# All matmuls of the main part of a fused attention and MLP layer as concurrent pairs of 64-row tiles

## The chip, the cores and the metric

The kernel runs on one core of one Trainium2 chip. The metric is the device time of one execution in microseconds (us). Each figure below is the median of several executions. A core has a TensorE (PE), which does the matmuls and writes to eight PSUM banks, and three elementwise engines: VectorE (DVE), ScalarE (ACT) and GpSimd (POOL). SyncE (SP) issues most DMAs.

## The reference, cut to what matters

```python
# S=2048 tokens, D=448, H=16 heads of Dh=28, F=1792
def _A_ref(x, wqkv, w_phi, wo):                      # linear attention
    q, k, v = ...(x @ wqkv)...
    pq = einsum("bhsd,hdf->bhsf", q, w_phi)          # pk likewise from k
    phi_q = concatenate([softmax(pq), softmax(-pq)]) # phi_k likewise
    kv  = einsum("bhsf,bhsd->bhfd", phi_k, v)        # "K-V"
    z   = einsum("bhsf->bhf", phi_k)
    num = einsum("bhqf,bhfd->bhqd", phi_q, kv)       # "numerators"
    den = einsum("bhqf,bhf->bhq", phi_q, z)[..., None] + 1e-6
    return (num / den)... @ wo

def _B_ref(x, w1, w2, w3, w4):                       # MLP with token shifts
    h  = gelu(layernorm(x) @ w1)
    hs = concatenate([four column blocks of h, shifted by 1, -1, 2, -2 tokens]) @ w2
    x1 = x + hs
    return x1 + gelu(layernorm(x1) @ w3) @ w4

xn = layernorm(x)
return x + _A_ref(xn, ...) + _B_ref(xn, ...)
```

## The kernel before

The kernel is one long unrolled program. A recorder takes every operation with what it reads and writes, and sets the semaphore waits: counters that hold an instruction back until the work it needs is done. Tokens are in 16 tiles of 128. D=448 is 3.5 times 128, so a product over D takes three matmuls with 128 rows (the contraction dimension lies on the rows) and one with 64. The 64-row ones, the *tails*, are issued in pairs on the upper and the lower half of the PE array, where they run at the same time (in the trace a pair's starts lie 3 ns apart).

The program has four stages:

1. The first 33.5 us or so: layer norm, transposes, V and W1 products. The change leaves them alone.
2. The K/Q loop, eight passes, from about 34 to 79 us. A pass makes K and Q products for two tiles and their exps on ACT. Then it makes W2 products, which DVE adds into `xn`, and K-V products of K tiles that DVE and POOL have normalised.
3. From the first W3 product on: the output stage. W3 products, Gelu on ACT, numerators, the division on DVE and POOL, a DMA transpose of the result `o`, and the W4 and `wo` products. DVE adds the residual ("fin_out").
4. The last two output tiles, in 128-row form before and after.

```python
def fulls(p, first, fills=()):            # 128-row matmuls
    for k in range(4):
        for kc in (0, 3, 2 - k % 2):
            R.mm(outs(k), lhs(k, kc, 0, 128), rhs(k, kc, 0, 128), ...)
        ...
def tails(p, first):                      # 64-row matmuls, even k rows 0-63, odd k rows 64-127
    for k in range(4):
        kc, lo = 1 + k % 2, 64 * (k % 2)
        R.mm(outs(k), lhs(k, kc, lo, lo + 64), rhs(k, kc, lo, lo + 64), first, not first)
def quad(p, fills=(), more=()):           # four banks: K/Q products, or W3 products
    fulls(p, True, fills)
    tails(p, False)
    for f in more: f()
def kv_tile(i):                           # 128 tokens on the rows
    for c in range(NC):
        R.mm(banks[6 + c // 2][...], vaug[:, i, 128*c:128*c+128], phik[:, i, :, CR*c:CR*c+CR], ...)
def num_tile(i):                          # 4 heads x 28 = 112 rows, 4 x 32 = 128 columns out
    for s in range(2):
        for c in range(NC):
            R.mm(bs[s][:, 128*c:128*c+128], eqT(g, c, s, ...), kvq[0:CR, 2*c+s, :], True, True)
    ...                                   # reciprocals, multiplies: DVE, then POOL
def fin_full(i):                          # 14 W4 and 3 wo matmuls with 128 rows; fin_tail(i): the 64-row one
    ...
plan = [ ...,
    [(N, 1), (O, 1), (Ff, 0), (G, 8), (G, 9), (N, 2), (O, 2)],   # what runs behind W3 quad 4
    ... ]
```

The softmax here doesn't subtract the row's maximum and nothing guards it: scores larger than these inputs give would overflow.

Of the kernel before, what the change touches and what calls it, by code (L numbers as in the profile page):

```python
# [17 lines left out]
class Recorder:  # L18
# [47 lines left out]
    def op(self, eng, fn, outs, ins, dma=False):  # L66
        w = set()
        r = set()
        for a in outs:
            w.update(self._keys(a))  # L70
        for a in ins:
            r.update(self._keys(a))
        self.ops.append((eng, fn, w, r, dma))

    def solve(self):
# [8 lines left out]
        for eng, fn, w, r, dma in self.ops:  # L84
# [21 lines left out]
            for k in w:  # L106
                if k in writers:
                    want(writers[k], False)
                if k in readers:
                    want(readers[k], False)  # L110
            kn = known[eng]
# [74 lines left out]

    def mm(self, out, lhsT, rhs, start, stop):
        self.op("PE", lambda e: e.matmul(out, lhsT, rhs, start=start, stop=stop, skip_group_check=True),  # L188
                [out], [lhsT, rhs])

    def tr(self, out, in_, ident):
        self.op("PE", lambda e: e.transpose(out, in_, ident), [out], [in_, ident])  # L192
# [16 lines left out]
def bass_parallel_sum__linear_kernel_hedgehog__mixer_s_mlp__prompt_kernel(  # L209
# [13 lines left out]
    with es:  # L223
# [42 lines left out]
        wpq = new("wpq", KC * D).rearrange("p (c d) -> p c d", c=KC)  # L266
# [8 lines left out]
        kvq = new("kvq", 8 * 128).rearrange("p (b e) -> p b e", b=8)  # L275
        kvT = view(w1_r, NC * 224).rearrange("p (c f) -> p c f", c=NC)
# [32 lines left out]
        def eqT(g, c, sgn, lo, hi):  # L309
            e = eq_lo if g < 2 else eq_hi  # L310
            return e[0:CR, c, sgn, 512 * (g % 2) + lo:512 * (g % 2) + hi]
# [49 lines left out]
        kq = kvq[0:CR, :, :].rearrange("p b (h e) -> p b h e", e=HP)  # L361
# [24 lines left out]
        def late_3():  # L386
            R.ew(pool, "memset", kvq[0:CR, :, :], 0.0)
            for b in range(8):
                R.ew(pool, "tensor_copy", kq[:, b, :, DH + 1:DH + 2], mb[:, :, 0:1])
# [47 lines left out]
        def fold(t, m, b):  # L437
            b = banks[b]
            for c in range(NC):
                R.mm(b[:, CR * c:CR * c + CR], wT[0:CR, t, c, START[m]:START[m] + 128], bd[0:CR, CR * c:CR * c + CR], True, True)  # L440
            dst = wpq if t == 0 else wpk
            R.ew(dve, "tensor_copy", dst[:, m, :], b[:, 0:D])
# [68 lines left out]
        def kq_quad(i, bs):  # L511
            g, c = divmod(i, 4)

            def outs(k):
                return banks[bs[k]][:, 0:D] if k < 2 else banks[bs[k]][0:CR, :]

            def lhs(k, kc, lo, hi):
                if k < 2:
                    return xnT[lo:hi, kc, 128 * (i + k):128 * (i + k) + 128]
                return wpq[lo:hi, kc, CR * (c + k - 2):CR * (c + k - 1)]  # L520

            def rhs(k, kc, lo, hi):
                return wpk[lo:hi, kc, :] if k < 2 else xnT[lo:hi, kc, 512 * g:512 * g + 512]

            quad((outs, lhs, rhs))
            for s in range(2):
                R.act(phik[:, i:i + 2, s, :], two(bs[0])[:, :, 0:D], ACT.Exp, scale=1.0 - 2.0 * s)
            e = (eq_lo if g < 2 else eq_hi)[0:CR, c:c + 2, :, 512 * (g % 2):512 * (g % 2) + 512]
            for s in range(2):
                R.act(e[:, :, s, :], two(bs[2])[0:CR, :, :], ACT.Exp, scale=1.0 - 2.0 * s)  # L530
# [10 lines left out]
        def kv_tile(i):  # L541
            for c in range(NC):
                R.mm(banks[6 + c // 2][:, 224 * (c % 2):224 * (c % 2) + 224].rearrange("p (s f) -> p s f", s=2),
                     vaug[:, i, 128 * c:128 * c + 128], phik[:, i, :, CR * c:CR * c + CR],
                     i == 0 and c % 2 == 0, i == NT - 1)

        def kv_copy():
            for h in range(2):
                R.ew(dve, "tensor_copy", kvT[:, 2 * h:2 * h + 2, :],
                     banks[6 + h][:, 0:448].rearrange("p (c f) -> p c f", c=2))  # L550

        def kv_blocks():
            b = banks[6]
            tv = tview(b, 1024).rearrange("p (b e) -> p b e", b=8)
            for c in range(NC):
                for s in range(2):
                    R.tr(tv[0:CR, 2 * c + s, :], kvT[:, c, CR * s:CR * s + CR], ident[:, :])
            R.ew(dve, "tensor_tensor", kq[:, :, :, 0:DH + 1],
                 tv[0:CR, :, :].rearrange("p b (h e) -> p b h e", e=HP)[:, :, :, 0:DH + 1],
                 mb[:, :, 0:1].unsqueeze(1).to_broadcast([CR, 8, 4, DH + 1]), op=ALU.mult)  # L560

        def w2_tile(i, b=None, stats=True):
            b = bank(4, 5) if b is None else banks[b]
            for m in range(NM):
                c0 = 2 + 128 * i - SHIFTS[m]
                R.mm(b[:, 0:D], hT[0:CR, m, c0:c0 + 128], w2[0:CR, m, :], m == 0, m == NM - 1)
            R.ew(dve, "tensor_tensor", xn[:, i, 0:256], b[:, 0:256], xn[:, i, 0:256], op=ALU.add)
            R.ew(dve, "tensor_tensor", xn[:, i, 256:D], b[:, 256:D], xn[:, i, 320:512], op=ALU.add)
            if stats:
                ln_stats(st2, mv2, xn, i)  # L570
# [8 lines left out]
        def num_tile(i):  # L579
# [3 lines left out]
            for s in range(2):  # L583
                for c in range(NC):
                    R.mm(bs[s][:, 128 * c:128 * c + 128], eqT(g, c, s, 128 * j, 128 * j + 128),
                         kvq[0:CR, 2 * c + s, :], True, True)
# [24 lines left out]
        def w3_quad(q, more=()):  # L611
            gf = [divmod(4 * q + k, FC) for k in range(4)]
            quad((lambda k: banks[k][:, :],
                  lambda k, kc, lo, hi: w3[lo:hi, kc, 128 * gf[k][1]:128 * gf[k][1] + 128],
                  lambda k, kc, lo, hi: gT[lo:hi, gf[k][0] % 2, kc, :]), (), more)
            for k in (0, 2):
                g, fc = gf[k]
                R.act(h3T[:, g % 2, fc:fc + 2, :], two(k), ACT.Gelu_apprx_tanh)
# [4 lines left out]
        def fin_bank(i):  # L623
            return (0 if i > 13 else 6 if i > 11 else 4) + i % 2

        def fin_full(i):
# [5 lines left out]
            for kc in (0, 3, 2 - i % 2, 1 + i % 2) if i >= NT - 2 else (0, 3, 2 - i % 2):  # L632
                R.mm(b[:, 0:D], oT[:, g % 2, kc, 128 * j:128 * j + 128], wo[:, kc, :], False, kc == 1 + i % 2)

        def fin_tail(i):
            g, j = divmod(i, 4)
            kc, lo = 1 + i % 2, 64 * (i % 2)
            R.mm(banks[fin_bank(i)][:, 0:D], oT[lo:lo + 64, g % 2, kc, 128 * j:128 * j + 128], wo[lo:lo + 64, kc, :],
                 False, True)
# [36 lines left out]
        order = list("102" * 3 + "1021" + "021" * 3 + "012")  # L676

        def take(n):
            r = [int(order.pop(0)) for _ in range(n // 2)]
            return [2 * b + j for b in r for j in (0, 1)]  # L680

        w2s = {0: (0, 1, 2, 3), 1: (4, 5), 2: (6, 7), 4: (8, 9), 5: (10, 11), 6: (12,), 7: (13,)}
        kvs = {1: (0,), 2: (1,), 3: (2, 3), 4: (4, 5), 5: (6, 7), 6: (8, 9), 7: (10, 11, 12)}
        for ps in range(8):
            kq_quad(2 * ps, take(4))
            todo = [(kv_tile, i) for i in kvs.get(ps, ())]
            if ps > 1:
                todo[0][0](*todo.pop(0)[1:])
            if ps == 3:
                alone(v_parts(12, take(4)), (todo,))  # L690
            else:
                b = take(2)
                for i in w2s[ps]:
                    w2_tile(i, b[i % 2], False)
                    for f in todo[0:1]:
                        f[0](*f[1:])
                    todo = todo[1:]
                for f in todo:
                    f[0](*f[1:])
            k_norm(2 * ps)  # L700
            for i in w2s.get(ps, ()):
                ln_stats(st2, mv2, xn, i)
                if i % 4 == 3:
                    ln_scale(mv2, rs2, i - 3, 4, 4)
# [5 lines left out]
        N, W, O, G, St, Ff, Fo = num_tile, w2_tile, o_T, g_T, store, fin_full, fin_out  # L710

        def ga(g):
            for j in range(4):
                g_apply(4 * g + j)

        def sc(g):
            ln_scale(mv2, rs2, 4 * g, 4, 4)

        plan = [
            [(kv_tile, 13), (W, 14), (kv_tile, 14), (g_apply, 7)],  # L720
            [(kv_tile, 15), (kv_copy,), (W, 15), (sc, 3), (G, 4), (G, 5)],
            [(kv_blocks,), (G, 6), (G, 7), (ga, 2)],
            [(N, 0), (O, 0)],
            [(N, 1), (O, 1), (Ff, 0), (G, 8), (G, 9), (N, 2), (O, 2)],
            [(N, 3), (O, 3), (Ff, 1), (G, 10), (G, 11)],
            [(N, 4), (O, 4), (Ff, 2), (St, 0), (N, 5), (O, 5), (Ff, 3), (St, 1)],
            [(ga, 3), (N, 6), (O, 6), (Ff, 4), (St, 2), (St, 3)],
            [(N, 7), (O, 7), (Ff, 5), (G, 12), (G, 13), (G, 14), (G, 15)],
# [57 lines left out]
```

## Time and profile before

| | before |
|---|---|
| median of 4 runs | 194.83 us (194.8 to 195.46) |
| span on the core | 193.6 us |
| first K product to first W3 product | 44.87 us |
| first K product to last matmul | 156.36 us |
| time in it beyond steady streaming | 10.04 us |
| of this, 48 changes of tiling mode | 4.53 us |

The last two rows come from start-to-start distances. In steady streaming a matmul starts a fixed time after the one before it: 216 ns for 512 columns, 189 ns for 448, 96 ns for 224, 56 ns for 128. What a distance has beyond that is called a *gap* here. I use gaps because matmuls overlap in the pipeline, so "busy" doesn't mean "at its peak".

From the page of the kernel before, its size, the busy time of each engine, and the chain of work that ended last, by engine:

```profile
span 193.6 us, 2935 instructions
PE 186.2 (96%) x1137; PEld 94.2 (49%) x1137; DVE 114.1 (59%) x271; ACT 78.1 (40%) x88; POOL 96.4 (50%) x149
PE 78%; DVE 7%; POOL 7%; ACT 3%; DMA 3%; issue 1%; ACTq 0%; DVEq 0%
```

PE is the bound: it is busy 96% of the span and holds 78% of the chain. The timeline of PE in the kernel before shows where it streams below its peak. A line has the start in us, the time from the first start to the last end, the engine, the output and inputs, rows\*columns of the weights, rows x moving columns, and how many matmuls were merged.

```profile
41.47 1.46 PE L188 MATMUL bank<-xnT,wpq 128*112 128x512 bf16 x6
42.86 0.36 PE L188 MATMUL bank<-wpk,xnT 64*128 64x448 bf16 x2
43.06 0.38 PE L188 MATMUL bank<-xnT,wpq 64*112 64x512 bf16 x2
43.38 0.93 PE L188 MATMUL bank<-w,hT 112*128 112x448 bf16 x4
```

These are two changes of tiling mode. The last of the six Q matmuls started at 41.47 + 1.46 - 0.38 = 42.55. The first 64-row matmul starts at 42.86, so 0.31 us later instead of 0.216. The pair of Q tails starts at 43.06, the next 128-row matmul 0.32 us later. Each change costs about 95 ns (92 to 96 in 46 of the 48; the other two 90 and 104). The second excerpt is from the output stage:

```profile
114.14 0.62 PE L188 MATMUL bank<-kvq,eq_lo 112*128 112x128 bf16 x8
114.24 1.16 DVE L200 TENSOR_TENSOR vaug<-bank,vaug 128x448 bf16<-128x448 f32 x2 [4.21 <-PE bank L188]
114.92 0.55 PE L188 MATMUL bank<-w,phik 128*128 128x448 bf16 x2 [0.17 <-DVE vaug L200]
```

Eight numerator matmuls take (0.62 - 0.22) / 7 = 57 ns each (0.22 is the length of one). After them the W4 products wait for the DVE adds that empty their bank. This happened five times, and cost 0.33 us each in start-to-start distance. The waits view of PE counts only the idle part that the modelled ends leave:

```profile
PE bank L188 <- DVE vaug L200: 0.8, 5, 0.2
PE bank L188 <- ACT phik L196: 0.7, 2, 0.4
PE bank L188 <- ACT eq_lo L196: 0.3, 1, 0.3
PE bank L188 <- POOL phik L200: 0.3, 1, 0.3
```

(Columns: us in total, times, longest.) Together 2.1 us idle, beside 4.5 us of mode changes, which no view lists as a wait.

### The profile page before, as it was taken

To read this page: it belongs to the slowest core of one execution; us is meant where nothing else is said; L and a number is where in the kernel's file an instruction comes from. 1 tells how busy PE (TensorE), PEld (TensorE's weight loads), DVE (VectorE), ACT (ScalarE), POOL (GpSimd) and SP (SyncE) were. 2 spreads that over 40 slices of the span, in tenths; PEclk is the share of its full clock that TensorE was granted. 3 is DMA by queue.
4 is the path that set the end of the run, shared out by engine and by line. 5 is a ranking of instruction groups with operands and counts; after the bars stand their busy time and mean duration, and the time that the engine had idled before them with its cause. 6 is when DMAs were issued, how large, how long until landed. Compare 5 with 4: busy or idle time off the path is not lost.

```text
span 193.6 us, 2935 instructions
## 1 busy us (share of the span) xinstructions
PE 186.2 (96%) x1137; PEld 94.2 (49%) x1137; DVE 114.1 (59%) x271; ACT 78.1 (40%) x88; POOL 96.4 (50%) x149
## 2 busy tenths in 40 slices
PE   7899999999999999999899999999999999999994
PEld 5445555444445555454344545444454445464451
DVE  5699655399989999835356436154172626655031
ACT  2349836846774667844550440124210440404000
POOL 5567830017877979973524414940444124376140
PEclk9999999999999999999999999999999999999999
DMA  5994259920011110121011343302263021122211
GB/s 171 352 214 91 53 95 366 350 80 0 0 32 27 27 27 0 37 48 27 0 30 30 79 83 29 76 0 75 54 85 78 24 51 40 42 51 68 61 47 47
DMA packets 32971, 14.74 MB, mean 76 GB/s; under 512 B 24702, under 2 KB 32446, under 8 KB 32958
## 3 DMA queue, kind: packets, MB, share of 16 engines
q1 hardware_dynamic: 31710, 13.58, 29.5%
q10 hardware_dynamic: 1248, 0.98, 1.6%
q8 instruction: 9, 0.15, 0.3%
q14 instruction: 4, 0.03, 0.1%
HBM read 7.08 MB, written 1.84 MB: 46 GB/s over the span
## 4 chain that ended last, share of the span: by engine, by line
PE 78%; DVE 7%; POOL 7%; ACT 3%; DMA 3%; issue 1%; ACTq 0%; DVEq 0%
PE bank L188 77%; POOL phik L200 3%; DMA xtok<-in_A_x_dram 3%; ACT phik L196 2%; DVE vaug L200 2%; DVE st L200 2%; POOL rs L200 2%; DVE xn L200 1%; DVE ksum L200 1%; ACT eq_lo L196 1%; POOL mv L200 1%; DVE mv L200 1%; PE bank L192 1%; ACTq L206 0%; POOL xn L200 0%
## 5 line engine op out<-in xcount | busy, mean ns | idle before, releaser
L196 ACT ACTIVATE phik<-bank 128x1024 bf16<-128x1024 f32 (+1 forms) x44 | 41.0, 984 | 85.3 <-PE bank L188 85.3
L200 DVE TENSOR_TENSOR vaug<-bank,vaug 128x464 f32<-128x464 f32 (+3 forms) x65 | 32.7, 513 | 31.3 <-PE bank L188 29.7
L188 PE MATMUL bank<-gT,w 128*128 128x512 bf16 (+1 forms) x224 | 46.1, 380 | 0.7 <-ACT phik L196 0.7
L188 PE MATMUL bank<-w,phik 128*128 128x448 bf16 x224 | 45.1, 353 | 0.8 <-DVE vaug L200 0.8
L200 POOL TENSOR_TENSOR xnT<-vaug 128x196 bf16<-128x196 f32 (+1 forms) x32 | 18.1, 585 | 49.5 <-DVE vaug L200 49.5
L200 POOL TENSOR_TENSOR phik<-phik,rks 128x896 bf16<-128x896 bf16 x16 | 26.8, 1696 | 21.1 <-DVE rks L200 21.0
L188 PEld LDWEIGHTS bank<-w,phik 128*128 128x128 bf16 x224 | 21.0, 98 | 20.2 <-DVE vaug L200 1.7
L188 PEld LDWEIGHTS bank<-gT,w 128*128 128x128 bf16 (+1 forms) x224 | 17.7, 97 | 24.7 <-issue 5.9
L200 POOL TENSOR_TENSOR vaug<-xn,xtok 128x448 f32<-128x448 bf16 x16 | 16.4, 1031 | 5.1 <-DVE vaug L200 5.1
L200 DVE RECIPROCAL vaug<-bank 128x16 f32<-128x16 f32 x16 | 4.1, 254 | 22.7 <-PE bank L188 22.7
L200 DVE TENSOR_REDUCE ksum<-phik 128x32 f32<-128x896 bf16 x16 | 16.8, 1052 | 0.0
L188 PE MATMUL bank<-xnT,wpq 128*112 128x512 bf16 (+1 forms) x64 | 14.9, 381 | 0.3 <-ACT eq_lo L196 0.3
L188 PE MATMUL bank<-wo,xnT 128*128 128x448 bf16 (+1 forms) x64 | 14.5, 352 | 0.0
L188 PE MATMUL bank<-xnT,w 128*112 128x512 bf16 (+1 forms) x64 | 14.3, 383 | 0.0
L188 PE MATMUL bank<-w,hT 112*128 112x448 bf16 x64 | 14.3, 353 | 0.0
L200 DVE TENSOR_TENSOR xn<-bank,xn 128x256 bf16<-128x256 f32 (+1 forms) x32 | 10.6, 378 | 5.6 <-PE bank L188 5.4
L188 PE MATMUL bank<-wpk,xnT 128*128 128x448 bf16 (+1 forms) x64 | 13.3, 354 | 0.0
L188 PE MATMUL bank<-wv,xnT 128*128 128x448 bf16 (+1 forms) x64 | 12.7, 353 | 0.1
L200 POOL TENSOR_SCALAR g_tok<-xn,rs 128x512 bf16<-128x512 bf16 x16 | 12.1, 767 | 0.0
L200 POOL TENSOR_TENSOR rs<-mv,mhalf 128x1 f32<-128x1 f32 (+2 forms) x16 | 11.3, 705 | 1.3
L196 ACT ACTIVATE hT<-bank 112x1024 bf16<-112x1024 f32 x8 | 7.9, 1027 | 5.8 <-PE bank L188 5.7
L200 DVE BATCH_NORM_STATS2 st<-xtok 128x6 f32<-128x448 bf16 x16 | 9.8, 610 | 0.6 <-DMA xtok<-in_A_x_dram 0.6
(61 smaller groups left out, 178.4 us busy)
## 6 DMA issues: line engine op xcount, KB each, us to landing
w<-in_B_w_dram SPq DMA_DIRECT2D x2, 896.0 KB, 5.7
out_dram<-vaug SPq DMA_DIRECT2D x15, 112.0 KB, 1.9
w<-in_B_w_dram SPq DMA_DIRECT2D x1, 1568.0 KB, 12.1
xtok<-in_A_x_dram SPq DMA_DIRECT2D x2, 448.0 KB, 8.1
xtok<-in_A_x_dram SPq DMA_DIRECT2D x2, 224.0 KB, 5.9
w<-in_B_w_dram ACTq DMA_DIRECT2D x2, 224.0 KB, 6.4
wo<-in_A_wo_dram SPq DMA_DIRECT2D x2, 224.0 KB, 6.8
w<-in_B_w_dram SPq DMA_DIRECT2D x1, 392.0 KB, 9.0
```

What stands on the lines that cost most here:

```text
L188: self.op("PE", lambda e: e.matmul(out, lhsT, rhs, start=start, stop=stop, skip_group_check=True), [out], [lhsT, rhs])
L192: self.op("PE", lambda e: e.transpose(out, in_, ident), [out], [in_, ident])
L196: self.op("ACT", lambda e: e.activation(out, in_, func, **kw), [out], [in_] + aps)
L200: self.op(eng, lambda e: getattr(e, name)(out, *args, **kw), [out], aps)
```

## The change

The intent is to leave the 64-row mode only once. Every product is split into a lower tile (rows 0 to 63) and an upper tile (rows 64 to 127). The two run at the same time on two banks: in the *first half* the lower tile works for bank A and the upper for bank B, in the *second half* they swap. Mode changes from the first K product on fall from 48 to 2. Three other things come with it:

- The recorder now keeps two row tiles from writing one bank at the same time. For this PE waits on its own semaphore, that is, for an earlier matmul of its own to be done, before a second half (the *own-semaphore wait*); the plan puts other work between the halves to cover that.
- Q is padded to 32 rows per head. A 64-row tile then holds just two heads, and a numerator matmul has 64 columns instead of 128.
- Both banks of a pair are complete only at the end of the second half, so what empties them starts later.

```diff
+            if eng == "PE":                       # recorder: order two row tiles on one bank
+                if tile[1] != mode[0]:
+                    mode = (tile[1], mode[1] + 1)
+                for k in w:
+                    for lo, (i, m) in tiles.setdefault(k, {}).items():
+                        if lo != tile[0] and m == mode[1]:
+                            need["PE"] = max(need.get("PE", -1), i)
+                    tiles[k][tile[0]] = (pos["PE"], mode[1])
...
+        def row_pairs(first, second, start=False):
+            for s, (p, q) in enumerate(zip(first, second)):
+                for out, lhs, rhs in (p, q):
+                    R.mm(out, lhs, rhs, start and s == 0, False)
+        def lap_pair(outs, lhs, rhs):             # K, Q, V and W3 products
+            def side(k, rows, kcs):
+                return [(outs[k], lhs(k, kc, *rows), rhs(k, kc, *rows)) for kc in kcs]
+            return (lambda: row_pairs(side(0, LO, (0, 1, 2, 3)), side(1, HI, (0, 1, 2, 3)), True),
+                    lambda: row_pairs(side(1, LO, (0, 1, 3)), side(0, HI, (0, 2, 3))))
...
-        def kv_tile(i): ...
+        def kv_half(i, late):
+            ...
+            a, b = side(LO, (2, 3) if late else (0, 1)), side(HI, (0, 1) if late else (2, 3))
+            row_pairs(a, b, i == 0 and not late)
...
-        def num_tile(i): ...
+        def num_half(i, late):
+            for c in range(NC):
+                for k, (lo, hi) in enumerate((LO, HI)):
+                    s = 1 - k if late else k
+                    at = 128 * c + 64 * k
+                    R.mm(banks[6 + s][:, at:at + 64], eqT(g, c, s, ...)[lo:hi, :], kvq[lo:hi, 2 * c + s, :], True, True)
...
+        def fin_pair(i):          # f1, f2: W4 halves of two tiles; f3, f4: wo halves, then both fin_outs
...
+        for ps in range(8):       # a pass of the K/Q loop
+            k[0](); q[0](); k[1](); q[1]()          # [joined here]
+            kq_exp(2 * ps, bk, bq)
+            for a in w: a[0]()                      # W2 first halves
+            for i in mine: kv_half(i, False)
+            for n, a in enumerate(w): a[1](); ...   # W2 second halves, then DVE adds
+            if ps < 7:
+                for i in mine: kv_half(i, True)
...
+        play([                    # a: W3 first half, b: second half and Gelu, n1/n2: numerator halves, kv: K-V half
+            a(0), kv(10, True), kv(11, True), kv(12, True), b(0), a(1), (wl[0],), b(1), kv(13, False), (w2_last,),
...
+            a(11), n1(3), b(11), n2(3), f(1, 1), a(12), n1(4), b(12), n2(4), f(2, 1), S(0, 1),
...
+            a(26), a(27), b(26), n1(14), b(27), n2(14), f(1, 6), S(10, 11), n1(15), f(2, 6), n2(15),
+            S(12, 13)])
```

For the last pair (`i == NT - 4`) `f1` also runs `f3`, and `f2` also runs `f4`.

## The prediction

> **What bounds it now.** The page shows PE busy for 186.2 of 193.6 us and PE holding 78% of the chain of waits. Busy time alone would not prove it, so I took start-to-start distances of matmuls from the timeline. From the first K product (34.06 us) on, nearly all lie at a steady 189 ns (448 columns), 216 ns (512), 96 ns (224) or 56 ns (128): 146.7 us in all. The rest is about 10 us:
> - 48 changes between 128-row and 64-row matmuls. Each lengthens one distance by about 95 ns (216 to 312 going in, 216 to 309 coming out): 4.5 us. The Trainium skill, "TensorEngine Tiling (Array Packing)", Key Properties, says that a mode change drains the array; the trace agrees.
> - Waits for other engines, some 4.3 us in 13 places: about 2.1 us before 92 us (exps, normalised K tiles), 2.2 us after (five waits of 0.33 us for the last bank's output add, one each for Gelu and for the K-V blocks).
>
> From 38 to 82 us DVE is nearly saturated too (about 5.45 us per pass of the K/Q loop, whose period is 5.44), so that stage has two bounds.
>
> **What the change does.** Matmul columns stay the same: the tails already ran as 64-row pairs (starts 3 ns apart, next pair at the full distance, no excess after the first), so pairs should sustain 189/216 ns.
> - Removed: about 46 mode changes, 4.4 us.
> - Numerator tiles stream 64 columns instead of 128. Eight matmuls take 0.445 us today; eight pairs should take 0.24 to 0.45, depending on what the weight loads sustain: 0 to 3.3 us, I take 1.6.
> - Both output banks are finished together and evacuated earlier relative to the next use: the five 0.33 us waits go, 1.6 us.
> - Added: PE waits on its own semaphore before the other row tile may write a bank (same page, Gotcha 1). Last start plus 379 ns plus about 60 to 90 ns must have passed. Where only a numerator half or one K-V half lies between (some 12 + 5 places), I expect 50 to 200 ns each: about 1.5 us. Elsewhere the filler (0.4 to 0.9 us) hides it.
> - Added in the K/Q loop: in the first pass the second W2 pair goes into the bank pair that the K exps still read (about 0.45 us), W2 evacuations start about 2 us later (two pairs finish together), and DVE, saturated, hardly catches up. I estimate 3 to 5 us of new waits there, against 2.3 us of mode changes saved in it.
> - The last numerator tile comes late: DVE chain 2.3 us, POOL 1.1, transpose 2.5, against about 6.3 us of filler: 0 to 1 us.
>
> **On the critical path.** In the output stage (after about 90 us) PE is the bound, so the saving counts in full: about 3.5 us net. In the K/Q loop DVE gives the gain back and more: 1 to 2.5 us lost.
>
> **Prediction.** 193.0 us, 8 in 10 between 189.5 and 196.5. Faster by over 2%: 0.22; within 2%: 0.69; slower: 0.09.
>
> **What would show it.** Right: start-to-start distances of pairs 189/216 ns without 310 ns steps; the part after 90 us shorter by 2 to 5 us; the K/Q loop not shorter, with waits for DVE xn or vaug and ACT; small PE waits before each second half behind a numerator half. Wrong: pairs slower than 195/222 ns (then slower overall), or the K/Q loop shorter than 44.9 us (34.06 to 78.92).
>
> **What would make it wrong.** Weight loads of two tiles not hiding in long runs of pairs; the own-semaphore wait costing far more or nothing; the DVE delay in the first pass being absorbed, which would give about 190.

## The result, and the profile after

| | before | after |
|---|---|---|
| median | 194.83 us | 191.61 us (191.38 to 191.99) |
| ratio | 1 | 0.9827 (95% interval 0.9807 to 0.9846) |
| span on the core | 193.6 us | 190.2 us |
| first K product to first W3 product | 44.87 us | 45.89 us |
| first K product to last matmul | 156.36 us | 152.92 us |
| gaps in it | 10.04 us | 9.39 us |

The outputs agree with the reference. A ratio is the mean time of one kernel's fast runs over that of the other's of the same rounds, so it is not quite the ratio of the quoted medians.

From the page of the changed kernel, the lines that answer to those of before:

```profile
span 190.2 us, 4514 instructions
PE 179.5 (94%) x1915; PEld 95.0 (50%) x1915; DVE 114.1 (60%) x278; ACT 79.3 (42%) x88; POOL 95.5 (50%) x143
PE 65%; DVE 12%; POOL 8%; DMA 7%; ACT 5%; issue 2%; ACTq 0%; DVEq 0%; POOLq 0%
```

PE lost 6.7 us of busy time but the span only 3.4. Its share of the chain fell from 78% to 65%: part of the gain has become waiting for the other engines. Start-to-start distances give this balance from the first K product on:

| | before | after |
|---|---|---|
| streaming of numerators | 7.12 | 3.70 |
| all other steady streaming, against before | | -0.2 |
| mode changes | 4.53 | 0.19 |
| waits for the output add (fin_out) | 1.64 | 0 |
| waits in the K/Q loop, up to the first W3 product | 1.78 | 4.85 |
| PE's own-semaphore waits in the output stage, 13 places | 0 | 1.40 |
| wait for the transpose of `o` at 107 us | 0 | 0.73 |
| wait for the last numerator tile | 0 | 1.30 |
| other gaps | 2.1 | 0.9 |

The gaps fell by 0.65 us and the streaming by 3.63. Against that, a tile sometimes ran without its partner, which I estimate at 0.9 us from the time with one tile streaming alone (2.11 us after, 0.31 before, counted half). The sum, -3.4 us, is what the first-K-to-last-matmul time shows (156.36 to 152.92).

The timeline of PE in the changed kernel, in the output stage, shows the new numerators and the new waits:

```profile
121.05 1.06 PE L203 MATMUL bank<-gT,w 64*128 64x512 bf16 x8
121.91 0.32 PE L203 MATMUL bank<-kvq,eq_lo 64*128 64x64 bf16 x8
122.17 0.82 PE L203 MATMUL bank<-gT,w 64*128 64x512 bf16 x6
122.83 0.28 PE L203 MATMUL bank<-kvq,eq_lo 64*128 64x64 bf16 x8
122.94 0.73 PE L203 MATMUL bank<-w,phik 64*128 64x448 bf16 x6
```

The second numerator half starts at 122.83 and what follows at 122.94: four pairs in 0.11 us, 29 ns per pair in the finer record. So a whole tile takes 0.23 us where it took 0.45. The first numerator half is the only work between the two halves of a W3 pair. The last W3 pair of the first half started at 121.735. Its 216 ns and the 117 ns of numerators end at 122.07, but the second half begins at 122.17: about 0.1 us is lost to the own-semaphore wait. This happens 13 times, 104 to 110 ns each (12 times before a second W3 half, once before a second W4 half).

The waits view of PE in the changed kernel, from 34 to 194 us (the three longest):

```profile
PE bank L203 <- POOL phik L215: 1.9, 2, 1.3
PE bank L203 <- DMA xnT<-xnT: 1.7, 2, 1.1
PE bank L203 <- ACT phik L211: 0.8, 2, 0.4
```

The five waits for the output add are gone. New are two long ones for POOL's normalised K tiles and two for a transpose of `o`. The timeline of the first pass shows how they begin (the bracket tells the idle time and its releaser):

```profile
36.80 1.73 ACT L211 ACTIVATE phik<-bank 128x896 bf16<-128x896 f32 x2 [0.45 <-PE bank L203]
37.06 1.10 PE L203 MATMUL bank<-w,hT 64*128 64x448 bf16 x8
38.58 2.44 PE L203 MATMUL bank<-w,hT 64*128 64x448 bf16 x24 [0.41 <-ACT phik L211]
40.31 1.88 DVE L215 TENSOR_TENSOR xn<-bank,xn 128x256 bf16<-128x256 f32 x6 [5.43 <-PE bank L203]
41.05 0.36 PE L203 MATMUL bank<-wpk,xnT 64*128 64x448 bf16 x1
```

The second W2 pair must wait until the K exps have left its banks (38.58). All W2 sums are complete only behind that, so DVE, idle for 5.43 us, gets its first W2 sum at 40.31; and the K products of the next pass wait for DVE (41.05). The chain of waits of the changed kernel (start, us, what) shows where this delay comes back:

```profile
56.59 7.62 PE bank L203 x88
64.22 1.28 DVE xn L215 x4
...
72.29 3.35 POOL phik L215 x2
...
79.79 8.29 PE bank L203 x90
...
102.08 5.08 DMA xnT<-xnT
107.21 71.86 PE bank L203 x875
```

PE's W2 products at 64 us release DVE's add, DVE then makes K sums, POOL normalises, and PE gets the last K tile at 79.79, after 1.50 us of waiting. From 107.21 to 179 the chain is PE alone: there a PE saving should count in full (e2 and e7 test it). Ahead of that stands a transpose that took 5.08 us.

### The profile page after: what moved, and what is told of

It reads as the page before. It is cut to its first block, busy times and chain, and to the rows that moved or that the text cites. A ratio compares the mean times of both kernels' runs of the same rounds, so it can differ in the third digit from the quotient of the medians.

```text
span 190.2 us, 4514 instructions
## 1 busy us (share of the span) xinstructions
PE 179.5 (94%) x1915; PEld 95.0 (50%) x1915; DVE 114.1 (60%) x278; ACT 79.3 (42%) x88; POOL 95.5 (50%) x143
## 4 chain that ended last, share of the span: by engine, by line
PE 65%; DVE 12%; POOL 8%; DMA 7%; ACT 5%; issue 2%; ACTq 0%; DVEq 0%; POOLq 0%
PE bank L203 64%; DMA xnT<-xnT 4%; ACT phik L211 4%; POOL phik L215 4%; DVE xn L215 3%; DVE vaug L215 3%; DMA xtok<-in_A_x_dram 3%; DVE st L215 2%; DVE ksum L215 2%; POOL rs L215 2%; POOL xnT L215 1%; ACT eq_lo L211 1%; DVE mv L215 1%; DVE rks L215 1%; PE bank L207 1%
## 5 line engine op out<-in xcount | busy, mean ns | idle before, releaser
L203 PE MATMUL bank<-gT,w 64*128 64x512 bf16 x392 | 50.5, 377 | 0.2
L203 PE MATMUL bank<-w,phik 64*128 64x448 bf16 (+1 forms) x420 | 45.0, 349 | 0.0
L203 PEld LDWEIGHTS bank<-w,phik 64*128 64x128 bf16 (+1 forms) x420 | 20.8, 94 | 17.9
L203 PEld LDWEIGHTS bank<-gT,w 64*128 64x128 bf16 x392 | 18.6, 94 | 17.7 <-ACT phik L211 1.0
L203 PE MATMUL bank<-xnT,wpq 64*128 64x512 bf16 x112 | 15.5, 377 | 0.3 <-ACT eq_lo L211 0.3
L203 PE MATMUL bank<-wo,xnT 64*128 64x448 bf16 (+1 forms) x106 | 14.0, 350 | 1.7 <-DMA xnT<-xnT 1.7
L203 PE MATMUL bank<-w,hT 64*128 64x448 bf16 (+1 forms) x128 | 14.9, 349 | 0.4 <-ACT phik L211 0.4
L203 PE MATMUL bank<-wpk,xnT 64*128 64x448 bf16 x112 | 14.3, 350 | 0.3 <-DVE xn L215 0.2
L203 PE MATMUL bank<-wv,xnT 64*128 64x448 bf16 (+1 forms) x76 | 12.8, 352 | 0.5 <-ACT phik L211 0.4
L203 PE MATMUL bank<-phik,vaug 64*128 64x224 bf16 x128 | 9.4, 256 | 1.9 <-POOL phik L215 1.9
```

Source lines behind the costliest of these rows:

```text
L203: self.op("PE", lambda e: e.matmul(out, lhsT, rhs, start=start, stop=stop, skip_group_check=True), [out], [lhsT, rhs], tile=self._tile(lhsT))
```

## The experiments

All are edits of the changed kernel, all gave right results, and all ratios are against the kernel before on the same chip. "Against the changed kernel" means the difference of the two ratios, times 194.83 us. The starting theory: (1) mode changes cost PE 95 ns each in the output stage; (2) narrow numerators save 3.4 us of streaming, but short numerator halves no longer cover PE's own waits; (3) the K/Q loop is held by DVE and POOL. The rivals: the gain came mainly from other reordering, or the K/Q loop gained from the mode changes too.

| run | median us | ratio | first K to last matmul | gaps |
|---|---|---|---|---|
| before | 194.83 | 1 | 156.36 | 10.04 |
| changed | 191.61 | 0.9827 | 152.92 | 9.39 |
| e1_num128 | 192.85 | 0.9890 | 153.78 | 7.05 |
| e2_fullfin | 194.97 | 0.9997 | 156.21 | 12.86 |
| e3_kvfull | 193.07 | 0.9904 | 154.00 | 10.54 |
| e4_w2first | 190.81 | 0.9789 | 152.05 | 8.74 |
| e5_num15 | 189.84 | 0.9745 | 151.50 | 8.02 |
| e6_kv12 | 190.71 | 0.9790 | 152.51 | 9.04 |
| e7_hoist | 190.80 | 0.9777 | 151.56 | 8.13 |
| e8_best | 186.67 | 0.9576 | | |
| e9_best_again | 186.88 | 0.9590 | 148.09 | 4.77 |
| e10_best128 | 190.20 | 0.9778 | 151.08 | 4.35 |
| e11_kvsplit | 193.86 | 0.9925 | 155.53 | 12.04 |

The 95% intervals are within 0.004 of the ratio. e8's profiled execution was a slow one, so its trace gives no comparable distances. The second column from the right is the sharper measure, since the start of the first K product varies from profile to profile (33.5 to 34.8 us) with the same code before it.

### e1: numerators 128 columns wide again

```diff
-        kvq = new("kvq", 8 * 64)...
+        kvq = new("kvq", 8 * 128)...
-                    at = 128 * c + 64 * k
-                    R.mm(banks[6 + s][:, at:at + 64], eqT(...)[lo:hi, :], kvq[lo:hi, 2 * c + s, :], True, True)
+                    at = 128 * c
+                    R.mm(banks[6 + s][:, at:at + 128], eqT(...)[lo:hi, :], kvq[lo:hi, 2 * c + s, :], not late and c == 0, False)
```

> The changed kernel, but its numerator pairs stream 128 columns again (block-diagonal rows widened with zeros; result unchanged). Theory (most of the gain is the narrower numerators, 56 to 29 ns a pair, 16 tiles of 8 pairs): 3.4 us of streaming come back, of which up to 1.3 us may be hidden, because a wider first half fills the wait before the next second half (12 waits of about 109 ns): 2.1 to 3.4 us slower than the changed kernel, 193.7 to 195.0. Rival (the gain is the mode changes, and narrow pairs are bound by their weight loads): within 0.7 us of the changed kernel.

Measured: slower by 1.2 us (first K to last matmul +0.87). That is below the 2.1 of the theory and above the 0.7 of the rival, so both missed. The streaming came back as said, +3.41 us. But the gaps fell by 2.34, where I had allowed for 1.3: the own-semaphore waits went from 1.40 us to none, the 0.73 us wait at 107 us didn't occur, and small ones shrank. The 0.73 us need not be a cost of the narrow numerators: the transpose behind it took 4.00 us here instead of 5.08. The timeline of PE in this run, at the same place as above:

```profile
121.78 0.39 PE L203 MATMUL bank<-kvq,eq_lo 64*128 64x128 bf16 x8
122.01 0.82 PE L203 MATMUL bank<-gT,w 64*128 64x512 bf16 x6
122.66 0.39 PE L203 MATMUL bank<-kvq,eq_lo 64*128 64x128 bf16 x8
```

Four pairs of 128 columns take 122.01 - 121.78 = 0.23 us, which is four times 56 ns: no gap. So in the changed kernel about two thirds of what the narrow numerators save was eaten by new waits. If that reading is right, the same undoing must cost the full 3.4 us or nearly so where the waits are gone: see e10.

### e2: 128-row W4 and wo products, with their 40 mode changes

```diff
             def f1(): ...
-                row_pairs(up(0, LO), up(1, HI), True)
+                whole(up(0, (0, 128)), True)
             def f2():
-                row_pairs(up(1, LO), up(0, HI))
+                whole(up(1, (0, 128)), True)
             def f3():
-                row_pairs(att(0, LO, (0, 1, 2, 3)), att(1, HI, (0, 1, 2, 3)))
+                whole(att(0, (0, 128), (0, 2, 3)))
+                whole(att(1, (0, 128), (0, 1, 3)))
             def f4():
-                row_pairs(att(1, LO, (0, 1, 3)), att(0, HI, (0, 2, 3)))
+                row_pairs(att(0, LO, (1,)), att(1, HI, (2,)))
```

The recorder was also made to keep ordering two row tiles on one bank when a 128-row matmul lies between (so in e3 and e11).

> The changed kernel, but the output projections (w4 and wo) run as 128-row matmuls again, between 64-row work: about 40 mode changes come back in the output stage, nothing else is longer. Theory (PE bounds this stage, a change costs 95 ns): 3.3 to 4.0 us slower than the changed kernel, about 195.3. Rival (the changes overlapped with other waits): under 1.5 us.

Measured: slower by 3.3 us (first K to last matmul +3.29), as fast as the kernel before. The timeline of PE shows a change of mode behind the second numerator half (the place at 122.83 and 122.94 above, of an earlier tile):

```profile
102.62 0.28 PE L200 MATMUL bank<-kvq,eq_lo 64*128 64x64 bf16 x8
102.84 1.50 PE L200 MATMUL bank<-w,phik 128*128 128x448 bf16 x7
```

What follows the numerators starts after 0.22 us instead of 0.11. The trace has 42 mode changes in place of 2, so 40 more at 94 ns = 3.8 us. The 0.73 us wait at 107 us didn't occur here (its transpose took 2.47 us), which more than makes up the difference to 3.3. So in the output stage mode changes cost their full price. The rival, that the reordering made the gain, doesn't hold for this stage: its plan is kept here (only within a pair of tiles do the W4 and `wo` products follow each other by tile), and the changes alone take the gain back.

### e3: K-V products in 128-row form

```diff
-            a, b = side(LO, (2, 3) if late else (0, 1)), side(HI, (0, 1) if late else (2, 3))
-            row_pairs(a, b, i == 0 and not late)
+            if not late:
+                for c, m in enumerate(side((0, 128), (0, 1, 2, 3))):
+                    R.mm(*m, i == 0 and c % 2 == 0, False)
```

> The changed kernel, but the K-V products run as 128-row matmuls in the early slot: 18 mode changes come back, 14 of them in the K/Q loop. Theory (the loop is bound by the exps of the Q banks and by the chain K exps, DVE, POOL, and not by PE): most of the 1.7 us is absorbed, 0.2 to 0.9 us slower. Rival (PE bounds it): 1.4 to 1.7 us slower.

Measured: slower by 1.5 us, first K to last matmul +1.09; first K to first W3 product 45.89 to 47.10. My theory said that the loop, held by DVE and POOL, absorbs most of the mode changes (0.2 to 0.9 us in all). Its number fell. The rival's 1.4 to 1.7 holds by the whole time, but not by the sharper measure. And the run can't decide, since the edit does more than add 18 changes, 14 of them in the loop, 1.33 us. It moves all of a tile's K-V work ahead of the second half of W2, so W2 sums are complete about 0.38 us later; and in the last pass it brings 0.58 us of K-V work ahead of the first W3 product that stood behind its first half. Hence e11.

### e11: K-V in 128-row form, order kept

```diff
-            row_pairs(a, b, i == 0 and not late)
+            for c, m in enumerate(side((0, 128), (2, 3) if late else (0, 1))):
+                R.mm(*m, i == 0 and c % 2 == 0, False)
```

> The changed kernel, but each half of a K-V step (early and late slot) runs as two 128-row matmuls instead of two 64-row pairs: the same work in the same slots, so the order fault of e3 (all of K-V ahead of the second W2 half) is absent; 26 mode changes come back up to the first w3 matmul, about 10 after it. Theory (what PE waits for at K-V tile 12 is a chain over DVE and POOL that starts at the end of W2 in the fifth pass; changes before its start move it, later ones are absorbed, those after the first w3 matmul count in full): first K to first w3 matmul 0.8 to 1.2 us longer, last matmul 1.6 to 2.2 us later, about 193.5. Rival A (PE bounds the loop throughout): 2.3 us to the first w3 matmul and 3.3 us in all. Rival B (the loop absorbs all of it): 0 to 0.3 and about 1.0 us.

Measured: first K to first W3 product +1.24 us, where the 26 added changes ahead of it are 2.47 us. So about half is absorbed in the loop and half is not. The whole kernel is slower by 1.9 us and first K to last matmul by 2.6; that is more than expected, since a 1.27 us wait for a transpose of `o` at 177 us appeared in place of the 0.73 at 107. The chain of waits of this run, with the start-to-start distances, shows where changes are absorbed and where not:

```profile
56.54 13.77 PE bank L200 x128
70.33 1.28 DVE xn L212 x4
...
73.08 3.35 POOL phik L212 x2
...
80.57 13.25 PE bank L200 x114
```

The DVE and POOL work that PE waits for at 80.57 starts at the end of PE's own W2 products (70.33; in the changed kernel the chain leaves PE a pass earlier, at 64.22). What makes PE later before that point makes this work later too. Of the 26 changes 7 (0.66 us) lie behind that point, and the wait for the tile fell by 0.52 us, from 1.50 to 0.98. The other 0.75 us was absorbed ahead of it, by waits of the Q products for ACT's exps of an earlier pass: one fell from 0.46 us to 0.09, three of 0.12 us went. Together that is the half that is missing. So a wait takes up only what PE adds after it has released the work that it waits for. "PE waits for POOL here" was true, and yet PE time earlier in the same loop was not slack.

### e4: the first W2 pair of pass 0 ahead of the second Q half

```diff
             k[1]()
+            if ps == 0:
+                w0 = w2_pair(0, more[0]); w0[0]()
             q[1]()
+            if ps == 0:
+                w0[1](); w2_out(0, more[0])
```

> The changed kernel, but in the first pass the first W2 pair is finished (first half before the second Q half) before the second pair begins. Theory (the pair order of the first pass delays DVE and with it the whole loop): the waits at 38.6, 41.0 and 41.6 us (1.2 us together) fall to about 0.3, the wait for the first normalised K tile at 46.0 grows by some 0.3, the first w3 matmul comes 0.7 to 1.1 us earlier, and the whole is 0.6 to 1.1 us faster, about 190.7. Rival (the loop is bound elsewhere and absorbs it): under 0.3 us.

Measured: faster by 0.7 us (first K to last matmul -0.87). The timeline of PE in the first pass of this run:

```profile
36.35 1.11 PE L203 MATMUL bank<-w,hT 64*128 64x448 bf16 x8
37.11 1.00 PE L203 MATMUL bank<-xnT,wpq 64*128 64x512 bf16 x6
37.76 2.86 PE L203 MATMUL bank<-w,hT 64*128 64x448 bf16 x24
40.45 0.92 PE L203 MATMUL bank<-wpk,xnT 64*128 64x448 bf16 x8
```

The Q half and the first pair's second half now cover the K exps, and the next pass begins at 40.45 instead of 41.05. The waits at 38.6, 41.0 and 41.6 us shrank from 1.2 to 0.2 us. A part came back as a longer wait for the first normalised K tile (0.75 to 1.11 us).

### e5: an earlier start for the last numerator tile

```diff
-            ... f(1, 6), S(10, 11), n1(15), f(2, 6), n2(15),
+            ... f(1, 6), S(10, 11), n1(15), f(3, 6), n2(15), f(2, 6), f(4, 6),
```

(f1 and f2 of the last pair no longer carry f3 and f4.) The second half of the last numerator tile now follows four pairs of `wo` matmuls instead of all of f2 and f4, so it is done earlier.

> The changed kernel, but the last numerator tile is computed one step earlier: its halves lie around the first attention half of the pair of tiles 12 and 13. Theory (the 1.3 us gap before the last four matmuls is only the chain DVE, POOL, transpose of a tile that came too late): the gap vanishes in whole, 1.1 to 1.4 us faster than the changed kernel, about 190.4. Rival (another tile or DVE becomes the last): under 0.6 us.

Measured: faster by 1.6 us (first K to last matmul -1.42). Ahead of it, the end of the changed kernel's timeline, then that of this run:

```profile
182.51 2.81 PE L203 MATMUL bank<-w,phik 128*128 128x448 bf16 x14
182.62 1.13 POOL L215 TENSOR_TENSOR xnT<-vaug 128x280 bf16<-128x280 f32 x2 [4.61 <-DVE vaug L215]
183.98 1.20 SPq L218 DMA_TRANSPOSE xnT<-xnT  x1
186.46 0.93 PE L203 MATMUL bank<-wo,xnT 128*128 128x448 bf16 x4 [1.13 <-DMA xnT<-xnT]
```

```profile
181.76 2.81 PE L203 MATMUL bank<-w,phik 128*128 128x448 bf16 x14
184.41 0.92 PE L203 MATMUL bank<-wo,xnT 128*128 128x448 bf16 x4
```

In the changed kernel the last `wo` products wait for POOL and a transpose; here they follow the W4 products at once.

### e6: K-V of tile 12 behind the first W3 pair

```diff
-        kvs = {..., 7: (10, 11, 12)}
+        kvs = {..., 7: (10, 11)}
-            a(0), kv(10, True), kv(11, True), kv(12, True), b(0), a(1), (wl[0],), b(1), ...
+            a(0), kv(10, True), kv(11, True), b(0), kv(12, False), a(1), (wl[0],), kv(12, True), b(1), ...
```

> The changed kernel, but the first half of K-V tile 12 moves from before the first w3 half to after it. Theory (PE stood 1.5 us for POOL's normalisation of tile 12, and could have worked on w3): the first w3 matmul comes 0.8 to 0.9 us earlier (then the exps' bank holds it) and the whole gains 0.6 to 0.9 us, about 190.8. Rival (the Gelus, which follow the Q exps and the table load, set the pace there): the gain is lost again at the second w3 pair, under 0.3 us.

Measured: faster by 0.7 us by the ratio, first K to last matmul only -0.40. The first W3 product came 0.77 us earlier: the 1.50 us wait for POOL ahead of it became a 0.95 us wait for the K exps. Part was lost again at the transposed `o` tile (0.73 to 0.93 us).

### e7: five W3 first halves moved one place ahead

```diff
-            a(11), n1(3), b(11), n2(3), f(1, 1), a(12), n1(4), b(12), n2(4), f(2, 1), S(0, 1),
+            a(11), a(12), n1(3), b(11), n2(3), f(1, 1), n1(4), b(12), n2(4), f(2, 1), S(0, 1),
```

(and so for 15, 18, 21 and 24). A second half then has at least another W3 half between it and its first.

> The changed kernel, but five first halves of w3 are moved one place earlier, so that ten second halves no longer follow their first half after one numerator half alone. Theory (each of the 12 gaps of 109 ns is PE's wait on its own semaphore and nothing else): ten of them vanish, 0.8 to 1.1 us faster, about 190.6. Rival (PE would otherwise wait for DVE or the transposes): under 0.4 us.

Measured: faster by 1.0 us (first K to last matmul -1.36). Ten of the 13 own-semaphore waits are gone, 1.1 us, so they were the separation of the halves and nothing else, and here the PE time saved counted in full.

### e8, e9: all of these together, and a bit more

The kernel joins e4 to e6 and a fuller form of e7 that was meant to put 0.8 us or more between the halves everywhere (three places still have a numerator half alone, and wait 109 ns each in the trace of e9). W2 of pass 1 is also put around the second Q half, K-V of tile 0 moves to pass 2, and in pass 3 the second V pair starts after the K-V halves.

```diff
-        kvs = {1: (0,), 2: (1,), 3: (2, 3), ..., 7: (10, 11, 12)}
+        kvs = {2: (0, 1), 3: (2, 3), ..., 7: (10, 11)}
-            if ps == 0:                             # of e4
+            if ps < 2:
-            a(9), n1(2), b(9), n2(2), f(2, 0), a(10), f(3, 0), b(10), f(4, 0), G(10, 11),
+            a(9), n1(2), b(9), n2(2), f(2, 0), a(10), a(11), f(3, 0), b(10), f(4, 0), G(10, 11),
-            a(11), n1(3), b(11), n2(3), f(1, 1), a(12), n1(4), b(12), n2(4), f(2, 1), S(0, 1),
+            n1(3), b(11), a(12), n2(3), f(1, 1), n1(4), b(12), n2(4), f(2, 1), S(0, 1),
...
```

> The changed kernel with all these waits taken away: W2 pairs of the first two passes around the second Q half, K-V tiles 0 and 12 later, numerator tile 15 earlier, every second w3 half behind at least 0.8 us of other work, w3 first halves as filler before the attention halves. Theory (the saving of the change is real PE time, hidden behind new waits): gaps after 34 us fall from 9.4 to about 4 us, 3.5 to 5 us faster than the changed kernel, 186.5 to 188. Rival (the waits are the trace of other bounds, DVE and POOL): gains do not add, 189 or more.

> The kernel of e8_best unchanged, because the one execution that was profiled there ran with every matmul some 400 ns longer (471 us) and shows nothing of the schedule. Theory: 186.4 to 187.0 us as its three other executions; gaps of PE after 34 us 3.5 to 5 us. If the slow execution belongs to the kernel, it comes again.

Measured: 186.67 and 186.88 us, 4.1 to 4.2% faster than before and 4.6 to 4.9 us faster than the changed kernel. It beats both kernels. From the page of the second run:

```profile
span 185.1 us, 4517 instructions
PE 177.3 (96%) x1915; PEld 93.9 (51%) x1915; DVE 114.3 (62%) x278; ACT 79.3 (43%) x88; POOL 95.6 (52%) x143
```

Gaps fell from 9.39 to 4.77 us. Three waits near 0.9 us are left, all ahead of 80 us: for the Q exps at 46 us, for V copies on DVE at 59 us, and for K exps ahead of the first W3 product.

One of e8's four executions, the profiled one, took 472.63 us. It is left out of the ratio. Its page lists PE:

```profile
PE 466.7 (99%) x1915; PEld 169.0 (36%) x1915; DVE 115.3 (24%) x278; ACT 81.1 (17%) x88; POOL 95.4 (20%) x143
```

The other engines took their usual time, while every group of matmuls was longer: a 512-column pair came in the median every 620 ns instead of 216, a 448-column pair every 459 instead of 189. The listing gives its clock as 1.000, but its trace holds no record of the granted clock at all: alone of the 13 pages, this one has no PEclk line. So it can't be said what clock was granted. The same kernel ran four times in e9 without it, so it isn't a property of the kernel. It was one execution in the 48 of changed variants; its cause stays open.

### e10: e9 with numerators 128 columns wide

The edit is that of e1.

> The kernel of e8_best, but its numerator pairs stream 128 columns again, as in e1. Theory (in e1 the waits after a first half, 1.3 us, and other gaps took up two thirds of the 3.4 us of extra streaming; here almost no such gaps are left): 2.8 to 3.5 us slower than e8_best, about 189.8. Rival (wider pairs cost only some 1.2 us wherever they stand): under 1.8 us slower.

Measured: 3.3 us slower than e9 in the median (3.7 by the ratios, in which one execution of 191.70 at a granted clock of 0.991 counts), first K to last matmul +2.99. In e1 the same undoing cost 1.2 us. So the narrow numerators are worth their full streaming, 3.4 us less a little, once the waits that they brought are covered. The gaps differ by 0.4 us between e9 and e10, where between the changed kernel and e1 it was 2.34. That supports the reading of e1: the streaming costs its full price where there are no waits for it to fill.

## Why the prediction was right or wrong

The prediction gave 193.0 us with "within 2%" as most likely. The time was 191.61 us, 1.7% faster, inside the range of 189.5 to 196.5. Point by point, in its own terms:

- **PE is the bound, mode changes cost 95 ns.** Right. 46 changes removed gave 4.34 us in the balance, and e2 put 40 back for 3.3 us. The Trainium skill, "TensorEngine Tiling (Array Packing)", Key Properties, says that changing the mode drains the engine; the trace agrees with a stop at each change, of 90 to 104 ns.
- **Pairs sustain 189 and 216 ns.** Right: the streaming of all other products is unchanged but for 0.2 us.
- **Numerators: "0 to 3.3 us, I take 1.6".** Mis-sized, and the largest miss. The pairs ran at 29 ns, about half of 56, so streaming fell by 3.4 us. I had doubted that weight loads sustain it. The Trainium skill, "TensorE: Matmul & The Clock Gate", Part 2, Back-to-back issue gap, has N / 2.4 + 2.5 ns, which is 29.2 ns for 64 columns: used as an estimate it would have been right. But the same section says that it under-counts where a stream carries weight loads and columns are few, so the page alone could not have settled my doubt; the trace did.
- **The five 0.33 us waits go.** Right: 1.64 us.
- **PE's own waits, 50 to 200 ns in 12 + 5 places, 1.5 us.** Right in size: 13 places of about 0.11 us, 1.4 us. The K-V ones are near nothing (about 24 ns). The same tiling page, Gotcha 1: PSUM Pressure, says that different row tiles cannot access one bank at the same time and that software must synchronise; it has no cost for it, the trace has. No run here breaks the rule, so the runs show what keeping it costs and not the rule itself.
- **The K/Q loop is "1 to 2.5 us lost".** Right: 1.02 us to the first W3 product, and 0.58 us of K-V second halves were pushed behind it, so 1.6. Of its two terms, the new waits ("3 to 5 us") came to 3.1 us, and the mode changes saved ("2.3 us") only to 1.7, since just 18 of the 48 lay there. The first-pass wait that it named is there (0.57 us at 38.6), but the longest waits, 1.50 and 0.75 us, are for POOL's normalised K tiles, where it had expected DVE and ACT. DVE stands in that chain, as the prediction said, though it was busy for 5.1 to 5.3 us of three passes of the kernel before that I looked at (5.44 us each), and not for 5.45.
- **The last numerator tile, "0 to 1 us".** Slightly too small: 1.30 us.
- **"About 3.5 us net" in the output stage.** Too small: about 4.5 to 5, from the first-K-to-last total of -3.4 and the loop's loss of 1.0 to 1.6. This is the numerator term again (1.8 us more), about 0.6 us of mode changes that lay here and not in the loop, and other gaps that fell, less the 0.73 us wait at 107 us that was not foreseen and the longer wait at the end. That misses in both directions partly cancelled, and left the total this near, is luck.

A later expectation of mine failed, in e3: that the K/Q loop, waiting for DVE and POOL, would absorb mode changes. e11 shows that only about half is absorbed. The chain of waits explains the other half (PE's W2 products start the DVE and POOL work that PE waits for). The waits that shrank add up to what was absorbed; that each of the other changes delayed the chain by its full price is argued, not shown.

## What to carry to other kernels

Where TensorE holds the chain, count the changes of tiling mode in the timeline: no view lists them as waits, and here they were 95 ns each, 4.5 us in all. When a sum is split over two row tiles, put work between the two halves that outlasts the first half's finish (0.23 us of numerators was enough here, 0.12 was not), and check what the later completion of both banks does to the engines that empty them. A wait of TensorE for another engine is slack only from the point on where that engine's chain was started; set up a balance of streaming and gaps to see whether a gain was cancelled by new waits, as two thirds of the narrow numerators' gain was here.

## What the Trainium skill lacked or had wrong

- "TensorEngine Tiling (Array Packing)", Key Properties: no figure for a mode change. Here 90 to 104 ns each over 48 changes, 46 of them between 92 and 96.
- The same page, Gotcha 1: PSUM Pressure: no figure for ordering two row tiles on one bank. Here 104 to 110 ns with 0.117 us of other work between, none with 0.23 us (e1) or with 0.8 us (e9).
- "TensorE: Matmul & The Clock Gate", Part 2, Back-to-back issue gap: it gives some 81 ns (128 columns) and 131 ns (512 columns) per matmul as what a stream with weight loads sustains, and calls N / 2.4 + 2.5 an isolated gap that under-counts and over-counts. Here streams with a weight load for every matmul (the page lists as many of them as matmuls) ran at 56 ns and 216 ns, and 29 ns for pairs of 64-row tiles with 64 columns: the formula holds, the two figures don't.
- "Runtime: NRT & Kernel Launch", Instruction fetch mechanics: it calls the cost of a fetch mostly hidden and doesn't speak of other DMAs. Over nine traces (before, after, e1 to e7), of 288 DMA transposes after 50 us 75 took more than 3 us from issue to landing (3.9 in the median and 5.3 at most, where 2.4 is usual), and all 75 overlapped an instruction fetch; 33 overlapped one and weren't late, and 180 had none and weren't late. The changed kernel has 4514 instructions against 2935, and the page lists 15 fetch packets on the first instruction queue against 9. The transpose of 102.08 is one of them: 5.08 us, and 0.73 us of PE. That they coincide is shown, how one delays the other isn't.
- "TensorE: Matmul & The Clock Gate", Part 1, gives 426.7 ns for 512 columns on a cold array as the start-to-start distance; it also mentions one kernel whose cold matmuls lasted 617 ns on average in one run, without a cause. The slow execution of e8 ran pairs of 512 columns every 620 ns and of 448 columns every 459 ns in the median, 2.9 and 2.4 times the usual, so not at one ratio throughout; it has no record of the clock. No page describes such a state.
